# Squared-ReLU attention with a soft mixture of experts on one core: four relu buffers, the combine softmax in the logits' tile, and another order of loads and turns in the last chunks

## The chip, the cores and the metric

The kernel runs on one core of a Trainium2 chip. The time is device microseconds of one execution. Before the change the median of three runs is 1475.71 us (1475.2 to 1476.64). The profiled execution took 1476.88 us, and its span, from the first to the last instruction, is 1475.1 us: 1.8 us lie outside the span, and the profiled execution is 1.2 us above the median.

## The reference

```
scores = (z @ z.T) / S               # per batch: z is 2496 x 64, 8 batches
attn   = max(scores, 0) ** 2
x      = u * (attn @ v)              # 2496 x 256 per batch, 19968 tokens in all
logits = x @ phi                     # 19968 x 32, 8 experts with 4 slots each
d      = softmax of logits over the tokens     # one column per slot
slot_input = d.T @ x                 # 32 x 256
h      = max(slot_input[e] @ w1[e], 0)         # per expert, 256 -> 1024
slot_out[e] = h @ w2[e]                        # 1024 -> 256
c      = softmax of logits over the slots      # one row per token
out    = c @ slot_out                # 19968 x 256, float32
```

The softmax over the tokens is kept as a running maximum with rescaled sums, so that it can be added up while the tokens are still being made. The experts and the output need all tokens.

## The kernel before, in words

**Tiles.** Attention runs over 8 batches and, in each, over chunks of query tokens: five chunks of up to 512 tokens, and in the last batch chunks of 448, 512, 512, 512, 256 and 256. A chunk is named by its first token, so the last three are 18944 (512 tokens), 19456 and 19712 (256 tokens each). A chunk is five steps `p`, each over four blocks `kt` of 128 keys, and a step is two halves, which are called **slots** here: a chunk has ten slots. In each slot `between` runs first, then 24 matmuls `acc<-ph,v`, `acc<-pl,v` accumulate the chunk's output.

**What a slot carries.** `between` (L552) takes one task from the list `work`, then calls `pair`, which issues the scores of two key blocks for a slot three further on: six matmuls into two PSUM tiles `sc`, two relu on ACT into SBUF tiles `r` (L204), two squares in place, and on DVE per block a rounding copy `ph` and the rest `pl`. `run(middle)` (L207) puts pending ACT work between the relus and the squares, `run(behind)` (L216) puts pending DVE work behind the pair. Every engine executes in the order in which the program was written (`InOrder`), so this order is the schedule.

**The tasks.** 1024 finished tokens are a group `q` (0 to 19; group 18 is tokens 18432 to 19455, the last, 19, has 512). `groups(q)` (L303) returns its tasks: `blocks` turn the four quarters of `xg` into `y` (DVE `y<-xg`), `logits` runs matmuls `lg<-xg,phi_sb` and a DVE chain on `L`, with the exponentials `E` put in `middle`; `turn_e` turns `E` (DVE `y<-E`); four `shifts` are four DMAs each (`xt<-y`), issued by SP; `combine` and what follows make the softmax over the slots, the exponential again in `middle`; `slot_sums` multiplies the turned tokens, and `add_up` adds the product to `slot_acc` on DVE. In groups before 18 the sums ride with the next group's logits (`late`, `lg<-xt`). Group 18 is finished only when chunk 18944 is, so its tasks run one per slot through chunks 19456 and 19712. `between_last` (L518) turns part of the last tokens (`tr_last`) in the last two slots.

**Buffers and weights.** Keys and values of a batch take 15 of the 22 buffers of the pool `blk`. The expert weights are 32 tiles of 512 KB. Seven go to the buffers that are free in the last batch; eight follow in the last chunk, each into a block of keys or values that has been used up; ten go to a pool `wx` that takes over the space of the attention's working tiles, and seven more to `blk`. All DMAs are issued by SP, in program order, so a DMA that waits holds back all behind it.

**The end.** Behind the last chunk come the last group, layer 1 (`h<-w`), the turn of the hidden values (`hT`), layer 2 (`po<-w,hT`), and the output: 22 tiles `ot`, up to 1 MB each, made of `pf<-ch,soh` matmuls, copied by ACT and DVE and sent by SP (`outT<-ot`), 20.45 MB in all. The second half of layer 2 is spread among the first output tiles.

Of the kernel before, what the change touches and what calls it, by code (L numbers as in the profile page):

```python
# [8 lines left out]
F32 = mybir.dt.float32  # L9
# [7 lines left out]
P = 128  # L17
# [36 lines left out]
def attn_soft_moe_kernel(ctx, tc, uT, v, zz, phi, ww, outT):  # L54
# [125 lines left out]
    def scores(b, ch, p, w):  # L180


        j, o, n, t0 = ch
        k0 = 4 * p + 2 * w
        ps = [sc_ps.tile([P, QC], F32, tag="sc", name=f"sc_{t0}_{k0 + h}") for h in range(2)]
        if t0 == 0:
            for h, rows in enumerate(HALF):
                c = 2 * w + h
                pe.matmul(
                    ps[h], zraw[b, p][rows, c * P : (c + 1) * P], zraw[b, 0][rows],  # L190
                    start=True, stop=True,
                )
        else:
            zk, zq = zt[b, p], zt[b, j]
            for m, (kl, ql) in enumerate(((0, 0), (0, 1), (1, 0))):
                for h, rows in enumerate(HALF):
                    c = 2 * w + h
                    pe.matmul(
                        ps[h][:, :n], zk[rows, h ^ kl, c * P : (c + 1) * P],
                        zq[rows, h ^ ql, o : o + n], start=(m == 0), stop=(m == 2),  # L200
                    )
        rs = []
        for h in range(2):
            r = wa.tile([P, QC], F32, tag="r", name=f"r_{t0}_{k0 + h}", bufs=3)  # L204
# [61 lines left out]
    def finish_chunk(b, ch, acc):  # L266
        _, _, n, t0 = ch
        ut = ut_.pop(t0)
        s = 0
        while s < n:  # L270
            q, o = divmod(t0 + s, 1024)
            w = min(n - s, 1024 - o)
            if q not in xg_:
                xg_[q] = wk.tile([P, 2, 1024], F32, tag="xg", name=f"xg_{q}")
            for c in (slice(0, 1), slice(1, 2)) if t0 + n == N else (slice(0, 2),):
                dve.tensor_mul(xg_[q][:, c, o : o + w], acc[:, c, s : s + w], ut[:, c, s : s + w])
            if o + w == 1024:
                work.extend(groups(q))
            s += w

    late = []


    xt_last = [xt[:, t, 0:D] for t in range(4)]
# [18 lines left out]
    def groups(q):  # L303

        x = xg_.pop(q)
        L, E, lt = (
            wk.tile([P, 2 * P], F32, tag=t, name=f"{t}_{q}", bufs=1) for t in ("L", "E", "lt")
        )  # L310
        m = wk.tile([P, 5], F32, tag="m", name=f"m_{q}")
        rm = wk.tile([P, 2, 8], F32, tag="rm", name=f"rm_{q}")
        y = wk.tile([P, 4, NB], F32, tag="y", name=f"y_{q}", bufs=1)
        l8 = lt.rearrange("p (k s) -> p k s", s=NS)
        mnew, mold = runmax[q % 2], runmax[(q + 1) % 2]

        def logits():
# [10 lines left out]
                        )  # L328
            if late:
                late.pop()(ps)  # L330
            dve.tensor_copy(L, ps[:, 0, D : 2 * D])
            dve.tensor_add(L, L, ps[:, 1, D : 2 * D])
            if q == 0:
                dve.reduce_max(mnew, L, axis=AX.X)
            else:
                dve.reduce_max(m[:, 0:1], L, axis=AX.X)
                dve.tensor_max(mnew, m[:, 0:1], mold)
                dve.tensor_sub(m[:, 2:3], mold, mnew)
            dve.tensor_scalar_mul(m[:, 1:2], mnew, -1.0)
            middle.append(exps)  # L340

        def exps():
            act.activation(E, L, AF.Exp, bias=m[:, 1:2], accum_out=m[:, 4:5])
            if q:
                act.activation(m[:, 3:4], m[:, 2:3], AF.Exp)

# [1 line left out]

        def turn_block(j, c):
            dve.transpose(  # L350
                y[:, :, j * D : (j + 1) * D].rearrange("p b (t c f) -> p c t b f", t=4, c=2)[:, c],
                x[:, c, 512 * j : 512 * (j + 1)].rearrange("p (t b k) -> p t b k", t=4, b=4),
            )

        def turn_e():
            dve.transpose(
                y[:, :, 2 * D :].rearrange("p b (j s) -> p j b s", j=2),
                E.rearrange("p (j b k) -> p j b k", j=2, b=4),
            )


# [1 line left out]
            return rm[:, i].unsqueeze(2).to_broadcast([P, 8, NS])  # L363

        def combine():
            dve.transpose(lt, L)
            dve.tensor_reduce(rm[:, 0], l8, axis=AX.X, op=ALU.max)
            dve.tensor_sub(l8, l8, spread(0))

        def combine_exp():  # L370
            act.activation(lt, lt, AF.Exp)

        def combine_sum():
            dve.tensor_reduce(rm[:, 1], l8, axis=AX.X, op=ALU.add)
            dve.tensor_scalar_add(rm[:, 1], rm[:, 1], 1e-9)
            dve.reciprocal(rm[:, 1], rm[:, 1])
            dve.tensor_mul(l8, l8, spread(1))

        def combine_turn():
            dve.transpose(cw[:, 2 * q : 2 * q + 2].rearrange("p j n -> p (j n)"), lt)  # L380

        def slot_sums(ps):
            for j in range(2):
                for t in range(4):
                    o = 2 * D + j * NS
                    for h, rows in enumerate(HALF):
# [3 lines left out]
                            xt[rows, :, j * D + t * 64 : j * D + (t + 1) * 64],  # L390
                            start=(j == 0), stop=(j == 1),
                        )
            behind.append(lambda: add_up(ps))

        def add_up(ps):
            snew, sold = slot_acc[q % 2], slot_acc[(q + 1) % 2]
# [14 lines left out]
        shifts = [lambda a=a: shift(y, a) for a in range(4)]  # L411
        e, c0, c2, c3 = (lambda f=f: behind.append(f) for f in (turn_e, combine, combine_sum, combine_turn))
        c1 = lambda: middle.append(combine_exp)
        rest = lambda: None
        if q < NQG - 2:

            todo = [logits, *blocks, e, shifts[0], c0, shifts[1], c1, shifts[2], c2, shifts[3], c3]
            todo.append(lambda: late.append(slot_sums))
        else:


            todo = [*blocks[:2], logits, rest, *blocks[2:], e, *shifts, c0, c1, c2, c3, rest]
# [18 lines left out]
    def load_w(pool, tag):
        i = len(w_raw)
        if i < NW:
            t = pool.tile([P, 2, 512], F32, tag=tag, name=f"w_{i}")
            sp.dma_start(t, ww[i].rearrange("p (k n) -> p k n", k=2))
            w_raw.append(t)
# [35 lines left out]
    def loads(i, w):  # L482
# [6 lines left out]
        if b < B - 1:  # L489
            if j == NQ - 3 and w:  # L490
                landing.append(load_z(b + 1, p))
            m = -1
            if j == NQ - 2 and w:
                m = p - 1
            elif j == NQ - 1 and q in (1, 3, 5, 7, 8, 9):
                m = NQ - 1 + (1, 3, 5, 7, 8, 9).index(q)
            if m >= 0:
                landing.append(load_v(b + 1, m))
        elif t0 >= N - 512 - 256 and t0 < N - 256:
            if len(w_raw) < NBLK - 15:  # L500
                load_w(blk, "blk")
        elif t0 == N - 256 and q >= 2:
            load_w(blk, "blk")
        if i % (NQ * NP) == 0 and w == 0 and landing:
            behind.append(landing.pop(0))

# [6 lines left out]

        return opening_splits

    xps = []
# [31 lines left out]
    for i, (b, ch, p) in enumerate(steps):  # L548
# [315 lines left out]
```

## Time and profile before

| what | value |
|---|---|
| median of 3 runs | 1475.71 us |
| profiled execution | 1476.88 us |
| its span | 1475.1 us |
| PE busy | 1448.1 us, 98% |
| DVE busy | 1172.4 us, 79% |
| ACT busy | 980.7 us, 66% |
| weights `w<-in_w` | 32 DMAs of 512 KB |
| outputs `outT<-ot` | 22 DMAs of 512 KB to 1 MB |

The page's shares are means over stages that differ. Up to about 1354 us from the span's start the chunks have 512 queries; chunks 19456 and 19712 follow until 1397; layers 1 and 2 until about 1428; and the last 45 us are output. The change touches the stretch from about 1350 us on, so the views to read are those limited to a window there: the waits of each engine, the issues of SP, and the table of stretches with the share and the rate of the DMA engines. In a table of stretches the columns are the stretch and its length, busy time of each engine with the number of instructions, the granted TensorE clock, the share of time that the 16 DMA engines were busy, and GB/s. In a list of waits they are who waited for whom, the sum in us, how often, and the longest.

### The profile page before, as it was taken

The page shows a single profiled execution, that of the slowest core. Times are in us where ns is not written, and L with a number is a line of the kernel's source. Part 1 is how long each engine was busy: PE and PEld are TensorE (multiplying, and loading weights), DVE is VectorE, ACT ScalarE, POOL GpSimd, SP SyncE. Part 2 cuts the span into 40 slices and gives each one's busy share as a digit, 9 for nine tenths or more (in the row PEclk, how much of TensorE's full clock was granted, in tenths as well). Part 3 has the DMA queues.
Part 4 walks back from the last instruction along what each step waited for, and adds up shares of the span by engine and source line. Part 5 has one row for each costly group of instructions (what it writes and reads, how often), then busy time and mean ns, then how long its engine had stood idle before and what let it go on. Part 6 is the DMA issues. An engine that isn't in the chain of part 4 may idle for free.

```text
span 1475.1 us, 35858 instructions
## 1 busy us (share of the span) xinstructions
PE 1448.1 (98%) x13945; PEld 1206.1 (82%) x13945; DVE 1172.4 (79%) x2324; ACT 980.7 (66%) x1923; POOL 4.0 (0%) x22
## 2 busy tenths in 40 slices
PE   9999999999999999999999999999999999999985
PEld 6888989898987888789888888789888788878852
DVE  6878876888788887788778888798878888777754
ACT  7777766767667766677667676676767776655543
POOL 0000000000000000000000000000000000000000
PEclk9999999999999999999999999999999999999995
DMA  3013111132021302131112231121202130203599
GB/s 123 22 44 83 58 40 29 46 106 55 26 76 46 90 20 55 44 84 54 44 31 69 61 85 45 46 74 58 55 16 83 44 89 22 54 15 130 190 389 387
DMA packets 51243, 113.90 MB, mean 77 GB/s; under 512 B 8577, under 2 KB 11137, under 8 KB 49025
## 3 DMA queue, kind: packets, MB, share of 16 engines
q1 hardware_dynamic: 51072, 111.61, 24.2%
q8 instruction: 110, 1.80, 0.5%
q14 instruction: 61, 0.49, 0.1%
HBM read 68.71 MB, written 20.45 MB: 60 GB/s over the span
## 4 chain that ended last, share of the span: by engine, by line
PE 93%; DVE 3%; ACT 2%; DMA 1%; issue 1%; ACTq 0%; DVEq 0%; SPq 0%
PE acc L50 70%; PE sc L50 18%; PE lg L50 2%; PE pf L50 1%; ACT ot L50 1%; DMA w<-in_w 1%; DVE pl L50 1%; ACT r L50 1%; DVE ph L50 1%; PE h L50 0%; DMA outT<-ot 0%; DVE z L50 0%; DVE xg L50 0%; PE idle L50 0%; PE po L50 0%
## 5 line engine op out<-in xcount | busy, mean ns | idle before, releaser
L50 PE MATMUL acc<-ph,v 64*128 64x512 f32 (+2 forms) x6396 | 1023.7, 382 | 0.7 <-DVE v L50 0.6
L50 PEld LDWEIGHTS acc<-ph,v 64*128 64x128 f32 x6396 | 675.6, 184 | 102.9 <-issue 1.5
L50 ACT ACTIVATE r<-sc 128x512 f32<-128x512 f32 (+2 forms) x820 | 435.8, 574 | 435.0 <-PE sc L50 392.2
L50 PE MATMUL acc<-pl,v 64*128 64x512 f32 (+2 forms) x3198 | 696.2, 381 | 0.0
L50 DVE TENSOR_TENSOR pl<-r,ph 128x512 fp32r<-128x512 f32 (+5 forms) x820 | 546.3, 666 | 68.5 <-DVE ph L50 0.9
L50 DVE CAST ph<-r 128x512 fp32r<-128x512 f32 (+2 forms) x820 | 334.2, 408 | 158.8 <-ACT r L50 157.6
L50 ACT ACTIVATE r<-r 128x512 f32<-128x512 f32 (+2 forms) x820 | 454.4, 609 | 0.0
L50 PEld LDWEIGHTS acc<-pl,v 64*128 64x128 f32 x3198 | 374.2, 184 | 48.8
L50 PE MATMUL sc<-z,z 64*128 64x512 f32 (+2 forms) x1920 | 284.1, 382 | 1.2 <-ACT r L50 1.2
L50 PEld LDWEIGHTS sc<-z,z 64*128 64x128 f32 x1920 | 195.6, 185 | 41.6 <-issue 6.2
L50 PE MATMUL sc<-z 64*128 64x512 f32 (+2 forms) x480 | 70.3, 381 | 1.3 <-ACT r L50 1.3
L50 PEld LDWEIGHTS sc<-z 64*128 64x128 f32 x480 | 48.4, 185 | 10.2 <-ACT r L50 1.9
L50 DVE TENSOR_TENSOR v<-vr,v 128x512 fp32r<-128x512 f32 x80 | 53.5, 677 | 3.9 <-ACT v L50 3.7
L50 DVE STREAM_TRANSPOSE y<-xg 128x512 f32<-128x512 f32 x76 | 53.7, 706 | 0.6
L50 DVE TENSOR_TENSOR xg<-acc,ut 128x1024 f32<-128x1024 f32 (+7 forms) x57 | 48.8, 880 | 3.9 <-PE acc L50 3.9
L50 ACT CAST v<-vr 128x512 fp32r<-128x512 f32 x80 | 48.6, 617 | 2.1 <-DMA vr<-in_v 2.1
L50 DVE TENSOR_TENSOR z<-zr,z 64x512 fp32r<-64x512 f32 x70 | 48.0, 686 | 2.1
L50 ACT CAST z<-zr 64x512 fp32r<-64x512 f32 x70 | 43.4, 620 | 1.7
L50 DVE COPY ot<-pf 128x1024 f32<-128x1024 f32 (+2 forms) x22 | 24.3, 1104 | 23.0 <-PE pf L50 21.7
L50 ACT COPY ot<-pf 128x1024 f32<-128x1024 f32 (+2 forms) x22 | 20.1, 915 | 27.0 <-PE pf L50 25.5
L50 PE MATMUL pf<-ch,soh 32*128 32x512 f32 (+2 forms) x88 | 24.0, 596 | 10.4 <-ACT ot L50 10.3
L50 PEld LDWEIGHTS pf<-ch,soh 32*128 32x128 f32 x88 | 10.4, 252 | 22.0 <-ACT ot L50 20.2
(123 smaller groups left out, 376.8 us busy)
## 6 DMA issues: line engine op xcount, KB each, us to landing
xt<-y SPq DMA_DIRECT2D x304, 72.0 KB, 2.4
vr<-in_v SPq DMA_DIRECT2D x80, 256.0 KB, 3.4
w<-in_w SPq DMA_DIRECT2D x32, 512.0 KB, 8.5
outT<-ot SPq DMA_DIRECT2D x16, 1024.0 KB, 6.5
ut<-in_uT SPq DMA_DIRECT2D x31, 512.0 KB, 3.9
zr<-in_zz SPq DMA_DIRECT2D x35, 256.0 KB, 4.0
ut<-in_uT SPq DMA_DIRECT2D x8, 448.0 KB, 3.7
outT<-ot SPq DMA_DIRECT2D x4, 512.0 KB, 6.1
```

The source lines that it names most:

```text
L50: return lambda *a, **k: self.tc.keep_in_program_order(f(*a, **k))
```

## The change

Five edits. (1) The tiles `r` have four buffers where they had three. (2) The combine softmax works in `L` itself; the tile `lt` is gone, and `L`, `E`, `y` are allocated where they are first used. (3) Group 18 gets its tasks as soon as its first 512 tokens are finished, and the first two block turns go to the last two slots of chunk 18944; in turn the two last tasks of an earlier group are joined to one. Within chunk 19456 the order is now: pause, two block turns, pause, logits, pause, `turn_e`, shifts. (4) The sums of group 17 are added up behind the first shift, not behind the logits; those of group 18 are multiplied one slot sooner and added up a slot after that. (5) In the last chunk 13 blocks are taken for weights where it were 8, and they are loaded in the order of the table `w_order`, which is not the order of their numbers; the space `wx` then takes weights 20 to 29. The last tokens' first two turns go to PSUM tiles of the pool `sc`, where they went to the single tile of the pool `ms`.

```diff
-            r = wa.tile([P, QC], F32, tag="r", name=f"r_{t0}_{k0 + h}", bufs=3)
+            r = wa.tile([P, QC], F32, tag="r", name=f"r_{t0}_{k0 + h}", bufs=4)
...
             if o + w == 1024:
-                work.extend(groups(q))
+                work.extend(todo_.pop(q, None) or groups(q))
+            elif q == NQG - 2 and o + w == 512:
+
+                todo_[q] = groups(q)
+                work.extend([todo_[q].pop(0) for _ in range(2)])
             s += w
...
         def combine():
-            dve.transpose(lt, L)
-            dve.tensor_reduce(rm[:, 0], l8, axis=AX.X, op=ALU.max)
-            dve.tensor_sub(l8, l8, spread(0))
+            dve.transpose(L(), L())
+            dve.tensor_reduce(rm[:, 0], l8(), axis=AX.X, op=ALU.max)
+            dve.tensor_sub(l8(), l8(), spread(0))
...
-            behind.append(lambda: add_up(ps))
+            (behind if q < NQG - 3 else adding).append(lambda: add_up(ps))
...
-            todo = [logits, *blocks, e, shifts[0], c0, shifts[1], c1, shifts[2], c2, shifts[3], c3]
-            todo.append(lambda: late.append(slot_sums))
+            todo = [logits, *blocks, e, shifts[0], c0, shifts[1], c1, shifts[2], c2, shifts[3]]
+            todo.append(lambda: (c3(), late.append(slot_sums)))
         else:
-            todo = [*blocks[:2], logits, rest, *blocks[2:], e, *shifts, c0, c1, c2, c3, rest]
+            add = lambda: behind.append(adding.pop(0))
+            todo = [*blocks[:2], rest, *blocks[2:], rest, logits, rest, e, lambda: (shifts[0](), add()), *shifts[1:]]
+            todo += [c0, c1, c2, c3]
             todo.append(lambda: slot_sums(ms_ps.tile([P, 2, 512], F32, tag="ms", name=f"sl_{q}")))
+            todo.append(add)
...
+    NW0 = NBLK - 15
+    w_order = [(0,), (1,), (2,), (5, 6), (3,), (7, 8), (4,), (9, 10), (), (11, 12)]
...
-        elif t0 == N - 256 and q >= 2:
-            load_w(blk, "blk")
...
-        if k == 1:
-            xps.append(ms_ps.tile([P, 2, 512], F32, tag="ms", name="tr_last"))
         if k:
-            ps = xps[0][:, k - 1, 0:D]
+            ps = sc_ps.tile([P, QC], F32, tag="sc", name=f"tr_last_{k}")[:, 0:D]
...
             pair(i + 1, s)
+            if i >= len(steps) - NP:
+                if len(w_raw) == NW0:
+                    for _ in range(13):
+                        take_w(blk, "blk")
+                for k in w_order[2 * p + s]:
+                    load_w(NW0 + k)
...
-    for _ in range(NWX):
-        load_w(wx, "wx")
-    while len(w_raw) < NW:
-        load_w(blk, "blk")
+    for i in range(NW0 + 13, NW):
+        take_w(*((wx, "wx") if i < NW0 + 13 + NWX else (blk, "blk")))
+        load_w(i)
```

The queue of SP behind the last shift of group 18 and the last load of `ut`. In a row `w_7` is weight tile 7, and the brackets name the semaphores that the load waits for (`DMAHW` is a DMA eight issues earlier; `PE` the last matmul that read the block). Before:

```order
L50 DMA ut_19712_21109<-in_uT 128x2x256 [waits DMAHW0_49,DVE_49]
L50 DMA w_7_21111<-in_w 128x1024 [waits DMAHW1_49,PE_49]
L50 DMA w_8_21160<-in_w 128x1024 [waits DMAHW2_49,PE_49]
...
L50 DMA w_14_21483<-in_w 128x1024 [waits DMAHW0_49,PE_49]
L50 DMA w_15_21567<-in_w 128x1024 [waits DMAHW1_49,DVE_49,PE_49]
L50 DMA w_16_21569<-in_w 128x1024 [waits DMAHW2_49,DVE_49]
```

Now:

```order
L50 DMA ut_19712_21090<-in_uT 128x2x256 [waits DMAHW0_49,DVE_49]
...
L50 DMA w_9_21116<-in_w 128x1024 [waits DMAHW3_49,PE_49]
L50 DMA w_12_21119<-in_w 128x1024 [waits DMAHW4_49,PE_49]
L50 DMA w_13_21120<-in_w 128x1024 [waits DMAHW5_49,PE_49]
L50 DMA w_10_21117<-in_w 128x1024 [waits DMAHW6_49,PE_49]
...
L50 DMA w_15_21122<-in_w 128x1024 [waits DMAHW0_49,PE_49]
L50 DMA w_11_21118<-in_w 128x1024 [waits DMAHW1_49,PE_49]
L50 DMA w_16_21123<-in_w 128x1024 [waits DMAHW2_49,PE_49]
...
L50 DMA w_18_21125<-in_w 128x1024 [waits DMAHW4_49,PE_49,Activation_49]
L50 DMA w_19_21126<-in_w 128x1024 [waits DMAHW5_49,PE_49,Activation_49]
L50 DMA w_20_21559<-in_w 128x1024 [waits DMAHW6_49,DVE_49,PE_49]
```

The load that waits for the end of attention (on DVE and PE both) stood ninth behind `ut`; now it stands fourteenth, and the five that moved ahead of it wait for single blocks.

DVE around the finish of chunk 18944 (`xg_18<-acc_18944`) and up to the turn of the exponentials (`y_18<-E_18`), before; `y_18<-xg_18` is a block turn, `L_18<-lg_18` the copy of the logits, and the left-out rows are `ph` and `pl` of the blocks between, and short rows of the logits and the sum:

```order
L50 TENSOR_TENSOR xg_18_20066<-acc_18944_20068,ut_18944_20069 128x2x512
...
L50 STREAM_TRANSPOSE y_18_20563<-xg_18_20066 128x4x4x32
...
L50 STREAM_TRANSPOSE y_18_20563<-xg_18_20066 128x4x4x32
L50 COPY L_18_20558<-lg_18_20667 128x256
...
L50 SCALAR_TENSOR_TENSOR slot_acc1_84<-slot_acc0_83,m_17_19540,lg_18_20667 128x256
...
L50 STREAM_TRANSPOSE y_18_20563<-xg_18_20066 128x4x4x32
...
L50 STREAM_TRANSPOSE y_18_20563<-xg_18_20066 128x4x4x32
...
L50 STREAM_TRANSPOSE y_18_20563<-E_18_20559 128x2x4x32
```

Now:

```order
L50 STREAM_TRANSPOSE y_18_20473<-xg_18_20048 128x4x4x32
...
L50 STREAM_TRANSPOSE y_18_20473<-xg_18_20048 128x4x4x32
L50 TENSOR_TENSOR xg_18_20048<-acc_18944_20052,ut_18944_20053 128x2x512
...
L50 STREAM_TRANSPOSE y_18_20473<-xg_18_20048 128x4x4x32
...
L50 STREAM_TRANSPOSE y_18_20473<-xg_18_20048 128x4x4x32
...
L50 COPY L_18_20779<-lg_18_20746 128x256
...
L50 STREAM_TRANSPOSE y_18_20473<-E_18_20800 128x2x4x32
...
L50 SCALAR_TENSOR_TENSOR slot_acc1_84<-slot_acc0_83,m_17_19520,lg_18_20746 128x256
```

Two of the four block turns stand ahead of the finish of chunk 18944, all four ahead of the logits, and the rescaled sum of group 17 stands behind `y<-E`, where it stood ahead of it.

More of the change, by code (lines that the diff above doesn't have):

```diff
@@ L277, in finish_chunk @@
             if o + w == 1024:
-                work.extend(groups(q))
+                work.extend(todo_.pop(q, None) or groups(q))
+            elif q == NQG - 2 and o + w == 512:
+                todo_[q] = groups(q)
+                work.extend([todo_[q].pop(0) for _ in range(2)])
             s += w
-    late = []
+    late, adding, todo_ = [], [], {}
     xt_last = [xt[:, t, 0:D] for t in range(4)]
@@ L303, in groups, with own @@
     def groups(q):
[L307 to L310, printed above, removed]
+        x = xg_[q]
+        tiles = {}
+        def own(tag, *shape):
+            if tag not in tiles:
+                tiles[tag] = wk.tile([P, *shape], F32, tag=tag, name=f"{tag}_{q}", bufs=1)
+            return tiles[tag]
+        L, E, y = lambda: own("L", 2 * P), lambda: own("E", 2 * P), lambda: own("y", 4, NB)
         m = wk.tile([P, 5], F32, tag="m", name=f"m_{q}")
         rm = wk.tile([P, 2, 8], F32, tag="rm", name=f"rm_{q}")
-        y = wk.tile([P, 4, NB], F32, tag="y", name=f"y_{q}", bufs=1)
-        l8 = lt.rearrange("p (k s) -> p k s", s=NS)
+        l8 = lambda: L().rearrange("p (k s) -> p k s", s=NS)
         mnew, mold = runmax[q % 2], runmax[(q + 1) % 2]
@@ L330, in logits @@
                 late.pop()(ps)
-            dve.tensor_copy(L, ps[:, 0, D : 2 * D])
-            dve.tensor_add(L, L, ps[:, 1, D : 2 * D])
+            dve.tensor_copy(L(), ps[:, 0, D : 2 * D])
+            dve.tensor_add(L(), L(), ps[:, 1, D : 2 * D])
             if q == 0:
-                dve.reduce_max(mnew, L, axis=AX.X)
+                dve.reduce_max(mnew, L(), axis=AX.X)
             else:
-                dve.reduce_max(m[:, 0:1], L, axis=AX.X)
+                dve.reduce_max(m[:, 0:1], L(), axis=AX.X)
                 dve.tensor_max(mnew, m[:, 0:1], mold)
@@ L342, in exps @@
         def exps():
-            act.activation(E, L, AF.Exp, bias=m[:, 1:2], accum_out=m[:, 4:5])
+            act.activation(E(), L(), AF.Exp, bias=m[:, 1:2], accum_out=m[:, 4:5])
             if q:
@@ L350, in turn_block @@
             dve.transpose(
-                y[:, :, j * D : (j + 1) * D].rearrange("p b (t c f) -> p c t b f", t=4, c=2)[:, c],
+                y()[:, :, j * D : (j + 1) * D].rearrange("p b (t c f) -> p c t b f", t=4, c=2)[:, c],
                 x[:, c, 512 * j : 512 * (j + 1)].rearrange("p (t b k) -> p t b k", t=4, b=4),
@@ L356, in turn_e @@
             dve.transpose(
-                y[:, :, 2 * D :].rearrange("p b (j s) -> p j b s", j=2),
-                E.rearrange("p (j b k) -> p j b k", j=2, b=4),
+                y()[:, :, 2 * D :].rearrange("p b (j s) -> p j b s", j=2),
+                E().rearrange("p (j b k) -> p j b k", j=2, b=4),
             )
@@ L365, in combine @@
         def combine():
-            dve.transpose(lt, L)
-            dve.tensor_reduce(rm[:, 0], l8, axis=AX.X, op=ALU.max)
-            dve.tensor_sub(l8, l8, spread(0))
+            dve.transpose(L(), L())
+            dve.tensor_reduce(rm[:, 0], l8(), axis=AX.X, op=ALU.max)
+            dve.tensor_sub(l8(), l8(), spread(0))
         def combine_exp():
-            act.activation(lt, lt, AF.Exp)
+            act.activation(L(), L(), AF.Exp)
         def combine_sum():
-            dve.tensor_reduce(rm[:, 1], l8, axis=AX.X, op=ALU.add)
+            dve.tensor_reduce(rm[:, 1], l8(), axis=AX.X, op=ALU.add)
             dve.tensor_scalar_add(rm[:, 1], rm[:, 1], 1e-9)
             dve.reciprocal(rm[:, 1], rm[:, 1])
-            dve.tensor_mul(l8, l8, spread(1))
+            dve.tensor_mul(l8(), l8(), spread(1))
         def combine_turn():
-            dve.transpose(cw[:, 2 * q : 2 * q + 2].rearrange("p j n -> p (j n)"), lt)
+            dve.transpose(cw[:, 2 * q : 2 * q + 2].rearrange("p j n -> p (j n)"), L())
         def slot_sums(ps):
@@ L410, in groups @@
         blocks = [lambda j=j, c=c: behind.append(lambda: turn_block(j, c)) for j in range(2) for c in range(2)]
-        shifts = [lambda a=a: shift(y, a) for a in range(4)]
+        shifts = [lambda a=a: shift(y(), a) for a in range(4)]
         e, c0, c2, c3 = (lambda f=f: behind.append(f) for f in (turn_e, combine, combine_sum, combine_turn))
@@ L438, in split_lo, with take_w, load_w @@
         parts[k].append(lo)
[L441 to L446, printed above, removed]
+    def take_w(pool, tag):
+        w_raw.append(pool.tile([P, 2, 512], F32, tag=tag, name=f"w_{len(w_raw)}"))
+    def load_w(i):
+        sp.dma_start(w_raw[i], ww[i].rearrange("p (k n) -> p k n", k=2))
     w_raw = []
+    NW0 = NBLK - 15
+    w_order = [(0,), (1,), (2,), (5, 6), (3,), (7, 8), (4,), (9, 10), (), (11, 12)]
     def load_u(b, ch):
@@ L499, in loads @@
         elif t0 >= N - 512 - 256 and t0 < N - 256:
-            if len(w_raw) < NBLK - 15:
-                load_w(blk, "blk")
-        elif t0 == N - 256 and q >= 2:
-            load_w(blk, "blk")
+            if len(w_raw) < NW0:
+                take_w(blk, "blk")
+                load_w(len(w_raw) - 1)
         if i % (NQ * NP) == 0 and w == 0 and landing:
@@ L514, in loads @@
         return opening_splits
-    xps = []
     def between_last(k):
-        if k == 1:
-            xps.append(ms_ps.tile([P, 2, 512], F32, tag="ms", name="tr_last"))
         if k:
-            ps = xps[0][:, k - 1, 0:D]
+            ps = sc_ps.tile([P, QC], F32, tag="sc", name=f"tr_last_{k}")[:, 0:D]
             turn_x(ps, xg_[NQG - 1], k - 1)
@@ L556, in between @@
             pair(i + 1, s)
+            if i >= len(steps) - NP:
+                if len(w_raw) == NW0:
+                    for _ in range(13):
+                        take_w(blk, "blk")
+                for k in w_order[2 * p + s]:
+                    load_w(NW0 + k)
             if 2 * i + s + 3 >= 2 * len(steps):
@@ L572, in attn_soft_moe_kernel @@
     wx = exx.enter_context(tc.tile_pool(name="wx", bufs=NWX, side="right", reuse_waits="tile"))
-    for _ in range(NWX):
-        load_w(wx, "wx")
-    while len(w_raw) < NW:
-        load_w(blk, "blk")
+    for i in range(NW0 + 13, NW):
+        take_w(*((wx, "wx") if i < NW0 + 13 + NWX else (blk, "blk")))
+        load_w(i)
     q = NQG - 1
@@ L591, in attn_soft_moe_kernel @@
     E = wk.tile([P, 2 * P], F32, tag="E", name="E_last", bufs=1)[:, 0:P]
-    lt = wk.tile([P, 2 * P], F32, tag="lt", name="lt_last", bufs=1)[:, 0:P]
+    lt = wk.tile([P, 2 * P], F32, tag="L", name="lt_last", bufs=1)[:, 0:P]
     nc.gpsimd.memset(tiny[:, 0:512], 0.0)
@@ L602, in attn_soft_moe_kernel @@
     pm = sc_ps.tile([P, QC], F32, tag="sc", name="pm")
-    xq = ms_ps.tile([P, 2, 512], F32, tag="ms", name="tr_last_1")
+    xq = ms_ps.tile([P, 2, 512], F32, tag="ms", name="tr_last")
     ep_, tp = (acc_ps.tile([P, 2, QC], F32, tag="acc", name=n) for n in ("et_sums", "et_last"))
```

## The prediction

> **What bounds the kernel now.** The page first: PE is busy 98% of the span, so nearly all of it is matmuls at their own pace, and a gain is to be looked for only where that ends. The table of stretches (the columns are named in its head) shows where.
>
> ```profile
> core 0: us, PE busy (x) PEld busy (x) DVE busy (x) ACT busy (x) POOL busy (x), PEclk, DMA share, GB/s
> 1000.00:1300.00 300.00, 300.00 (x2915) 254.16 (x2913) 244.67 (x497) 201.75 (x402) 0.00 (x0) 1.00 0.18 51
> 1390.00:1395.00 5.00, 4.33 (x66) 3.79 (x64) 3.10 (x10) 1.66 (x5) 0.00 (x0) 1.00 1.02 396
> 1395.00:1400.00 5.00, 5.00 (x63) 3.82 (x59) 1.83 (x7) 1.21 (x5) 0.00 (x0) 1.00 0.77 277
> 1400.00:1405.00 5.00, 4.67 (x42) 2.29 (x44) 3.07 (x13) 2.82 (x7) 0.00 (x0) 1.00 0.92 325
> 1405.00:1410.00 5.00, 5.00 (x49) 1.31 (x41) 4.93 (x7) 3.85 (x6) 0.00 (x0) 1.00 1.03 417
> 1420.00:1425.00 5.00, 4.17 (x78) 2.50 (x74) 2.08 (x3) 1.66 (x3) 0.00 (x0) 1.00 0.86 345
> 1425.00:1430.00 5.00, 4.45 (x76) 2.64 (x71) 2.56 (x3) 2.72 (x3) 0.00 (x0) 1.00 0.91 375
> 1430.00:1435.00 5.00, 3.01 (x23) 1.62 (x24) 3.56 (x3) 2.62 (x4) 0.00 (x0) 0.76 1.01 418
> 1460.00:1465.00 5.00, 3.53 (x36) 1.97 (x28) 2.45 (x2) 2.09 (x3) 0.00 (x0) 0.50 1.00 415
> ```
>
> Up to 1300 us PE has no gap, and the edits that reach back there (the fourth buffer, the shared tile, the joined tasks) can win nothing in that part. From 1390 the DMA engines are full (share about 1, some 415 GB/s) but for two dips: at 277 and 325 GB/s they leave (138 + 90) / 415 x 5 = 2.7 us unused between 1395 and 1405, and at 345 and 375 another 1.3 us between 1420 and 1430. So the end is a DMA stage of weights and outputs, and two things set it: when SP can feed it, and when the first outputs are there. The issues of SP say why the first dip is there (start, length, what, how many):
>
> ```profile
> 1372.93 10.87 SPq L50 DMA_DIRECT2D xt<-y  x16
> ...
> 1383.90 0.53 SPq L50 DMA_DIRECT2D ut<-in_uT  x1
> 1384.53 4.63 SPq L50 DMA_DIRECT2D w<-in_w  x8
> ...
> 1397.37 7.03 SPq L50 DMA_DIRECT2D w<-in_w  x10
> ...
> 1424.93 0.33 SPq L50 DMA_DIRECT2D outT<-ot  x1
> ...
> SPq L50 <- DVE y L50: 13.3, 1, 13.3
> ```
>
> SP waits 13.3 us for `y`, then needs 10.87 us to issue 16 shifts, then sends eight weights by 1389.2 and nothing until 1397.37, the end of attention. Eight weights and `ut` are 4.5 MB, 11 us at 415 GB/s: they have run dry when the next ones come. Why `y` is late is in the groups and waits of DVE between 1354 and 1394, the two chunks of 256:
>
> ```profile
> L50 DVE TENSOR_TENSOR pl<-r,ph 128x256 fp32r<-128x256 f32 x33 | 14.0, 425 | 2.6
> L50 DVE CAST ph<-r 128x256 fp32r<-128x256 f32 x35 | 9.9, 283 | 2.7 <-ACT r L50 2.2
> L50 DVE STREAM_TRANSPOSE y<-xg 128x512 f32<-128x512 f32 x4 | 2.8, 705 | 0.0
> ...
> DVE ph L50 <- ACT r L50: 2.2, 4, 1.1
> ...
> ACT r L50 <- DVE pl L50: 3.4, 8, 0.8
> ACT lt L50 <- DVE lt L50: 1.5, 1, 1.5
> ...
> PE sc L50 <- ACT r L50: 1.4, 4, 0.5
> PE tr_last L50 <- DVE slot_acc L50: 0.6, 1, 0.6
> ...
> PE po L50 <- DMA w<-in_w: 1.7, 3, 0.8
> ```
>
> DVE waited only 2.2 us for relus and squares in these 40: it works back to back, and ACT (3.4 us in 8 waits) waits for it because a third relu tile is still being read. In this stretch DVE, not PE, sets the pace, and PE loses 1.4 us to relus and 0.6 to the sum of group 18.
>
> **The change part by part.** Sums are made against the profiled execution's own span, 1475.1 us; its time was 1476.88, and the median of the runs is 1475.71, so the change of the span is laid on the median.
>
> *Block turns and the late sum.* Before `y<-E` can run, DVE now has less ahead of it.
>
> ```profile
> 1353.07 0.30 DVE L50 CAST ph<-r 128x256 fp32r<-128x256 f32 x1 [1.46 <-ACT r L50]
> ...
> 1362.95 0.29 DVE L50 CAST ph<-r 128x256 fp32r<-128x256 f32 x1 [1.07 <-ACT r L50]
> ...
> 1364.29 0.47 DVE L50 SCALAR_TENSOR_TENSOR slot_acc<-slot_acc,m,lg 128x256 f32<-128x256 f32 x1
> ...
> 1364.81 0.42 DVE L50 TENSOR_TENSOR slot_acc<-slot_acc,lg 128x256 f32<-128x256 f32 x1
> 1365.14 0.29 DVE L50 CAST ph<-r 128x256 fp32r<-128x256 f32 x1
> ...
> 1372.43 0.45 DVE L50 STREAM_TRANSPOSE y<-E 128x256 f32<-128x256 f32 x1
> ```
>
> The first turn falls into the 1.46 us that DVE idles before 1353.07; of the second the cover is gone, since it stands in the back-to-back stretch, ahead of `xg`. That takes 0.70 us off the stretch. The sum of group 17 (1364.29 to 1365.14: 0.85 us with its small third part) moves behind `y<-E`. Together `y` is ready 1.55 us sooner. The shifts keep their 10.87 us, so `ut` and the first weight follow 1.55 us sooner. What is late next: the sum, one chunk on, has nobody waiting for it until group 18's. The logits come two slots later with the same chain and the same 1.07 us of DVE idle behind the exponentials: no gain, no loss, as `y<-E` stands two slots behind them still.
>
> *Four relu tiles.* The trace has no run with four. The bounds are 0 (DVE, with the same work, takes the time back) and the whole 1.4 us that PE waited for relus. I take 0.95: the waits behind the two exponentials remain in part, because ACT's 1.5 us for the combine (`lt`, now `L`) is a chain of dependent steps and not a lack of tiles.
>
> *The last tokens' turn* in the `sc` tiles no longer waits for `slot_acc`: 0.55 us (the row gives 0.6). So attention ends 0.70 + 0.95 + 0.55 = 2.2 us sooner, 0.55 at the least, 3.0 at the most (0.70 + 1.4 + 0.55, and a third of a us of short DVE waits).
>
> *Slot sums a slot sooner.* PE runs them in order, and they need the last shift. It is issued at 1383.1 (the end of the 16, less a sixteenth of 10.87) and lands 2.4 us later by the row `xt<-y` of the page's issues; 1.55 us sooner that is 1383.95, and the slot starts at 1386.34 less 0.70 and 0.95, 1384.7. It lies free by 0.7 us; without the earlier `y` PE would wait 0.8.
>
> ```profile
> xt<-y SPq DMA_DIRECT2D x304, 72.0 KB, 2.4
> ...
> 1386.34 0.62 PE L50 MATMUL sc<-z,z 64*128 64x256 f32 x6
> ```
>
> *Weights.* Thirteen instead of eight between the shifts and the end of attention, in the order in which blocks come free: the loads behind them no longer find a dry queue, and the 2.7 us dip is filled. A load whose block is late holds back the others, but with seven free at once (9 us of transfers) it has time. The weights are all there 1.55 + 2.7 = 4.25 us sooner. Sharing `L` and joining two tasks cost no instruction: nothing, below the matmuls.
>
> *From the end of attention to the outputs* the instructions are the same. Layer 2 waited three times, 1.7 us, for weights (row above); weights that come 4.25 us sooner for work that is 2.2 us sooner are there. So the third output, from which on the rate stays at 415 GB/s, is issued 2.2 + 1.7 = 3.9 us sooner than 1424.93. From there the stage is as long as it was: the second dip, before that output, stays. The chain of transfers (4.25) allows it, the chain of computation (3.9) decides: **1475.7 - 3.9 = 1471.8 us**.
>
> **The rivals.** *DVE keeps the pace.* If the fourth relu tile gives nothing and the block turn only moves the wait, attention ends 0.55 us sooner and the third output 2.25: 1473.5. For it: DVE's sum of work falls by only 0.70 us. Against it: waits of ACT on `pl` are eight, and spread. *The weights cover more.* If all of PE's waits go and attention ends 3.0 us sooner, the output is 4.7 sooner and the transfers' 4.25 decide, less a part of the second dip, which weights then fill: some 4.9, 1470.8, and at best with all of that dip 1470.2. *The shifts are not sooner* (PE or ACT is behind `y<-E`, not DVE): the queue starts as before, the slot sums wait 0.8 us, attention ends 1.4 us sooner, and the transfers gain 2.7 only: 1473.0.
>
> *Slower: the clock falls before the outputs begin.* The granted clock is 1.00 to 1430, 0.76 in the stretch from 1430 and 0.50 behind it, with PE busy 3.01 of 5 us where it falls. PE now gets less to wait for before the outputs, but comes to the sparse stage sooner. These rows lie between attention and the outputs:
>
> ```profile
> 1402.29 1.92 PE h L50 x16
> ...
> 1404.78 5.33 PE h L50 x48
> ...
> 1410.00 1.97 PE L50 MATMUL hT<-ident,hidden 128*128 128x128 f32 x16
> ...
> 1411.89 3.70 PE L50 MATMUL po<-w,hT 128*32 128x128 f32 x128
> ```
>
> At half the clock they would take up to 12.9 us more, 1471.8 + 12.9 = 1484.7; it decides from 3.9 us of them on, when the gain is eaten. Against it: the clock stayed at 1.00 through all of this stage. The Trainium skill, "TensorE: Matmul & The Clock Gate", Part 1, has the clock halve after one window of about 3.4 us in which PE idles and come back after one busy window. By that rule this rival needs such an idle window, and the rows show PE busy over half of every stretch, so it would not happen; but by these same rows the fall at 1430 to 1435 came with PE busy 3.01 of 5, so the trace does not bear the rule out as a full account.
>
> **How the numbers follow.** Forecast 0.55; weights cover more 0.16; DVE keeps the pace 0.12; shifts not sooner 0.10; slower, the clock or another loss of the same size, 0.07. A change under 0.2%, 2.95 us, can't be told from none here, which puts the line at 1472.8. Faster: the forecast, with a part of its spread beyond the line counted off, and the stronger case, 0.69; same: the two weak cases and that part, 0.24; slower 0.07. The range for 8 in 10 goes from 1469.4 (the strong case and 0.8 us for the spread of runs) to 1474.3 (both weak cases and 0.8).
>
> **What would show it.** Right: `y<-E` about 1.5 us before 1372.43 and the shifts with it; 13 weights between `ut` and the end of attention and no stretch of 5 us under 380 GB/s from 1387 to 1415; attention's last matmul about 2 us before 1397.3; no wait of `po` for `w`; fewer waits of ACT on `pl`; the third output near 1421. Wrong: `sl` waiting for `xt`; a new wait of SP for a block ahead of weights that are free; weights done well before the first output, with the DMA engines idle for longer than the second dip; a clock below 1.00 before 1420.

## The result, and the profile after

The changed kernel takes 1467.02 us (median of six runs, 1466.37 to 1467.45) where the kernel before took 1475.9 us beside it: a ratio of 0.9938, with a 95% interval of 0.9925 to 0.9951. That is 8.9 us, where 3.9 were forecast, and 1467.02 lies below the low end of the range. The profiled execution took 1466.37 us with a span of 1464.3. The spans differ by 10.8 us, 1.9 more than the medians, mostly since the profiled execution before lies 1.0 us above its median and the one after 0.65 below. One run of an experiment below, 1769.27 us at a granted clock of 0.747 where all other runs have 0.985 to 0.987, is left out of its ratio (the median there is 1472.48 with it and 1472.44 without).

The largest part of the 8.9 us was won before the place at which the prediction began to look. The timeline of PE shows the first scores of chunk 19456, with which the chunks of 256 queries begin; first the kernel before (start, length, what, how many), then the changed one:

```profile
1354.25 0.52 PE L50 MATMUL sc<-z,z 64*128 64x256 f32 x6
```

```profile
1348.13 0.52 PE L50 MATMUL sc<-z,z 64*128 64x256 f32 x6
```

These six matmuls come 6.12 us sooner. In the chunks of 512 little has changed: the number of relu tiles, the place of the combine softmax, and two tasks that are joined. The waits of ScalarE from 0 to 1300 us say what went away (engine, tile and whom it waited for: us in all, times, longest). Before:

```profile
ACT r L50 <- PE sc L50: 366.0, 311, 3.7
ACT r L50 <- DVE pl L50: 30.9, 48, 2.0
ACT r L50 <- PE acc L50: 3.0, 3, 1.6
```

After:

```profile
ACT r L50 <- PE sc L50: 401.0, 324, 3.5
```

With three tiles a relu had to wait 48 times, 30.9 us together, until VectorE had read the tile of three relus ago (`pl<-r,ph` is its last reader). With four there is no such wait. Most of them cost PE little or nothing, since scores are issued three slots ahead; some reach PE. One place shows how. The timeline before, from 290 to 299 us, of ScalarE, VectorE and PE (in square brackets the idle time before, and what ended it):

```profile
293.53 0.60 ACT L50 ACTIVATE r<-sc 128x512 f32<-128x512 f32 x1 [0.39 <-PE sc L50]
296.11 0.60 ACT L50 ACTIVATE r<-sc 128x512 f32<-128x512 f32 x1 [1.97 <-DVE pl L50]
```

```profile
292.44 0.44 DVE L50 STREAM_TRANSPOSE lt<-L 128x256 f32<-128x256 f32 x1
292.91 0.42 DVE L50 TENSOR_REDUCE rm<-lt 128x8 f32<-128x256 f32 x1
293.37 0.42 DVE L50 TENSOR_TENSOR lt<-lt,rm 128x256 f32<-128x256 f32 x1
293.71 1.22 DVE L50 TENSOR_TENSOR xg<-acc,ut 128x1024 f32<-128x1024 f32 x1
294.85 0.42 DVE L50 CAST ph<-r 128x512 fp32r<-128x512 f32 x1
295.30 0.69 DVE L50 TENSOR_TENSOR pl<-r,ph 128x512 fp32r<-128x512 f32 x1
```

```profile
292.64 0.96 PE L50 MATMUL sc<-z,z 64*128 64x512 f32 x6
...
296.14 0.39 PE L50 MATMUL sc<-z,z 64*128 64x512 f32 x1
296.76 0.96 PE L50 MATMUL sc<-z,z 64*128 64x512 f32 x5 [0.23 <-ACT r L50]
297.34 0.84 PE L50 MATMUL acc<-ph,v 64*128 64x512 f32 x4
```

At the end of a chunk VectorE has 2.4 us of other work in one piece (three steps of a combine softmax and `xg`, 292.44 to 294.9). It reads the old relu tile only from 294.85 to 295.99; the second relu of the pair, which could have followed the first at about 294.1, begins at 296.11; and the next scores, which need its PSUM tile, stop after one matmul. From the start of these six to the `acc` behind them are 1.20 us. The same place after the change:

```profile
292.71 0.63 PE L50 MATMUL acc<-ph,v 64*128 64x512 f32 x4
293.18 0.39 PE L50 MATMUL acc<-pl,v 64*128 64x512 f32 x2
293.41 0.86 PE L50 MATMUL sc<-z,z 64*128 64x512 f32 x6
294.11 0.63 PE L50 MATMUL acc<-ph,v 64*128 64x512 f32 x4
```

```profile
290.81 1.09 ACT L50 ACTIVATE r<-sc 128x512 f32<-128x512 f32 x2 [1.36 <-PE sc L50]
294.30 1.08 ACT L50 ACTIVATE r<-sc 128x512 f32<-128x512 f32 x2 [1.37 <-PE sc L50]
```

There it is 0.70 us, and both relus of a pair follow each other. The scores of this slot were 2.73 us sooner than before (293.41 for 296.14), the matmuls behind them are 3.23 sooner (294.11 for 297.34): one stall of 0.5 us. Of it the timeline counted 0.23 as a wait, and for all of 0 to 1300 us the waits of PE before give no more than this:

```profile
PE sc L50 <- ACT r L50: 1.0, 4, 0.3
```

What PE lost stands in another row, the waits of its weight loads (PEld) for the same relus, from 0 to 1300 us. Before, and after:

```profile
PEld sc L50 <- ACT r L50: 5.7, 13, 0.8
```

```profile
PEld sc L50 <- ACT r L50: 0.5, 2, 0.3
```

Three of the 13 and both of the two lie in the first 10 us. The other ten, 4.7 us in all, are at ten places between 55 and 1055 us, and with four tiles none of them is left. A single wait is not the exact loss: at 296.76 us the weight load waited 0.66 us where PE lost 0.5.

The lead of matching scores grows in such steps and some smaller ones: 2.2 us by 62 us of the kernel before, 2.7 by 262, 3.9 by 400, 5.0 by 745, 5.5 by 991, 6.1 by 1090. The first part of it is not won by the tiles. Some 0.8 us are there before a third relu has been issued; the second row of matmuls on `idle`, before and after, shows it:

```profile
5.84 1.03 PE L50 MATMUL idle<-cw 64*128 64x512 bf16 x8
```

```profile
5.05 1.03 PE L50 MATMUL idle<-cw 64*128 64x512 bf16 x8
```

In the eight experiments below this row begins anywhere from 4.86 to 5.86 us, the earliest with three tiles and one of the two latest with four, so it does not go with the number of tiles. From this row to the first scores of chunk 19456 it is 1348.3 to 1348.5 us in the four profiled executions with three tiles in the chunks of 512 (the kernel before among them), and 1343.0 to 1343.1 in the six with four or five. So the traces give the fourth tile 5.3 of the 6.12 us.

The rows by stretch, after (PE, PEld, DVE, ACT, POOL busy, then the granted clock, the DMA share, GB/s):

```profile
1000.00:1300.00 300.00, 300.00 (x2918) 248.63 (x2916) 244.87 (x495) 200.91 (x402) 0.00 (x0) 1.00 0.18 50
1385.00:1390.00 5.00, 5.00 (x74) 4.09 (x72) 1.72 (x6) 0.74 (x2) 0.00 (x0) 1.00 1.04 420
1390.00:1395.00 5.00, 4.56 (x49) 2.61 (x45) 2.96 (x14) 2.05 (x8) 0.00 (x0) 1.00 1.01 403
1410.00:1415.00 5.00, 4.82 (x100) 2.88 (x96) 2.37 (x4) 2.17 (x4) 0.00 (x0) 1.00 0.82 324
1415.00:1420.00 5.00, 4.07 (x74) 2.63 (x68) 3.62 (x3) 2.77 (x3) 0.00 (x0) 1.00 1.02 420
1420.00:1425.00 5.00, 2.85 (x34) 1.74 (x28) 2.65 (x3) 2.56 (x4) 0.00 (x0) 0.92 1.01 416
```

The first row is busy for 300.00 of 300 us, as it was before, though 0.6 us were won in that stretch. The first dip of the transfers is gone (every stretch between 1385 and 1410 has 403 GB/s or more); of the second (415 - 324) / 415 x 5 = 1.1 us are left.

The issues of SP from 1365 us on, in two windows, and the waits of PE from 1340 to 1465:

```profile
1365.25 10.64 SPq L50 DMA_DIRECT2D xt<-y  x16
1375.98 0.53 SPq L50 DMA_DIRECT2D ut<-in_uT  x1
1376.61 26.70 SPq L50 DMA_DIRECT2D w<-in_w  x25
1410.47 1.69 SPq L50 DMA_DIRECT2D outT<-ot  x2
...
1414.16 4.32 SPq L50 DMA_DIRECT2D outT<-ot  x3
```

```profile
PE pf L50 <- ACT ot L50: 11.1, 16, 0.9
PE po L50 <- ACT so L50: 1.2, 1, 1.2
PE sc L50 <- ACT r L50: 0.7, 1, 0.7
PE h L50 <- ACT tiny L50: 0.3, 1, 0.3
```

The shifts begin 7.68 us sooner (1365.25 for 1372.93), 1.56 more than the scores of chunk 19456. The third output, 1414.16, is 10.77 us sooner: 6.12 up to the first scores of chunk 19456, the 0.8 of the opening among them, and 4.65 from there on, where the forecast had 3.9. PE waits neither for weights in `po` nor for the sum of group 18 in `tr_last`.

### The profile page after: what moved, and what is told of

It is laid out like the page before. It is cut to its first block, busy times and chain, and to the rows that moved or that the text cites. A ratio compares the mean times of both kernels' runs of the same rounds, so it can differ in the third digit from the quotient of the medians.

```text
span 1464.3 us, 35841 instructions
## 1 busy us (share of the span) xinstructions
PE 1440.0 (98%) x13945; PEld 1169.9 (80%) x13945; DVE 1169.8 (80%) x2324; ACT 975.0 (67%) x1923; POOL 3.8 (0%) x22
## 4 chain that ended last, share of the span: by engine, by line
PE 96%; DMA 1%; DVE 1%; ACT 1%; issue 0%; ACTq 0%; DVEq 0%; SPq 0%; POOLq 0%
PE acc L50 72%; PE sc L50 19%; PE lg L50 2%; PE pf L50 1%; DMA outT<-ot 1%; ACT ot L50 1%; PE po L50 1%; PE h L50 0%; DVE pl L50 0%; PE idle L50 0%; DVE ot L50 0%; DVE ph L50 0%; ACT r L50 0%; PE hT L50 0%; PE et_sums L50 0%
## 5 line engine op out<-in xcount | busy, mean ns | idle before, releaser
L50 PE MATMUL acc<-ph,v 64*128 64x512 f32 (+2 forms) x6396 | 988.5, 382 | 0.7 <-DVE v L50 0.6
L50 ACT ACTIVATE r<-sc 128x512 f32<-128x512 f32 (+2 forms) x820 | 428.1, 574 | 432.4 <-PE sc L50 430.8
L50 PEld LDWEIGHTS acc<-ph,v 64*128 64x128 f32 x6396 | 605.2, 184 | 122.1 <-POOLq L253 1.4
L50 PE MATMUL acc<-pl,v 64*128 64x512 f32 (+2 forms) x3198 | 626.1, 381 | 0.0
L50 PEld LDWEIGHTS acc<-pl,v 64*128 64x128 f32 x3198 | 310.2, 184 | 57.9
L50 PE MATMUL sc<-z,z 64*128 64x512 f32 (+2 forms) x1920 | 265.2, 380 | 0.0
L50 PEld LDWEIGHTS sc<-z,z 64*128 64x128 f32 x1920 | 178.7, 184 | 41.1 <-issue 6.2
L50 PE MATMUL sc<-z 64*128 64x512 f32 (+2 forms) x480 | 66.6, 381 | 0.7 <-ACT r L50 0.7
L50 PEld LDWEIGHTS sc<-z 64*128 64x128 f32 x480 | 44.5, 184 | 10.8 <-issue 2.1
```

The source lines that it names most:

```text
L50: return lambda *a, **k: self.tc.keep_in_program_order(f(*a, **k))
```

## The experiments

Two theories stood before the first four. **A**: the fourth relu tile wins most of the time, in the chunks of 512 queries. **B**, the prediction's account: nothing is won there, and the gain is that of the last chunks. All times are medians, all ratios are to the kernel before on the same chip. An interval reaches 0.0008 to 0.0014 to either side, 1.2 to 2 us, so a difference of less than about 2 us between two changed kernels lies within the intervals and is told with the trace beside it.

| kernel | time, us | ratio, 95% interval |
|---|---|---|
| the change | 1467.02 | 0.9938, 0.9925 to 0.9951 |
| change, three relu tiles | 1473.61 | 0.9983, 0.9975 to 0.9992 |
| before, softmax in `L` | 1476.16 | 0.9999, 0.9990 to 1.0008 |
| before, softmax in `L`, four relu tiles | 1468.83 | 0.9953, 0.9939 to 0.9966 |
| change, eight weights as before | 1468.63 | 0.9949, 0.9936 to 0.9961 |
| change, fourth tile in the last chunks only | 1472.48 | 0.9973, 0.9964 to 0.9982 |
| change, old order of tasks | 1467.76 | 0.9945, 0.9933 to 0.9958 |
| change, last tokens' turns as before | 1467.11 | 0.9942, 0.9929 to 0.9956 |
| change, five relu tiles, nine `pl` | 1466.95 | 0.9940, 0.9927 to 0.9952 |

**Three relu tiles in the changed kernel**, all else as changed.

```diff
-            r = wa.tile([P, QC], F32, tag="r", name=f"r_{t0}_{k0 + h}", bufs=4)
+            r = wa.tile([P, QC], F32, tag="r", name=f"r_{t0}_{k0 + h}", bufs=3)
```

> The changed kernel with three relu tiles again, all else kept. Theory A: the fourth tile takes away ACT's waits for DVE in the chunks of 512 too (in the trace before, 31.2 us in 50 waits of ACT on pl up to 1340 us; in the trace after, none), and that is where 6.1 us of the gain lie, with some 1 us more in the chunks of 256. So 1467.0 + 7 = 1474 us, and the first scores of chunk 19456 come at about 1354 us from the span's start, not at 1348. Theory B, the prediction's own: the fourth tile is worth 0.95 us and the 6.1 us come from something else of the change, the shared tile or the joined tasks: 1468 us.

1473.61 us: one number takes back 6.6 of the 8.9 us, as A has it. The wait of ScalarE from 0 to 1300 us is back word for word:

```profile
ACT r L50 <- DVE pl L50: 30.9, 48, 2.0
```

and the scores of chunk 19456 begin at 1354.32, where they began before the change.

**The shared tile alone**: the kernel before, with the combine softmax in `L`.

```diff
-        L, E, lt = (
-            wk.tile([P, 2 * P], F32, tag=t, name=f"{t}_{q}", bufs=1) for t in ("L", "E", "lt")
-        )
+        L, E = (wk.tile([P, 2 * P], F32, tag=t, name=f"{t}_{q}", bufs=1) for t in ("L", "E"))
+        lt = L
...
-    lt = wk.tile([P, 2 * P], F32, tag="lt", name="lt_last", bufs=1)[:, 0:P]
+    lt = wk.tile([P, 2 * P], F32, tag="L", name="lt_last", bufs=1)[:, 0:P]
```

> The kernel before with the combine softmax in the logits' tile alone; three relu tiles. Theory A: the same instructions on the same engines, no time: 1475.9 us, within 1 us. Theory B: if the shared tile carries the 6.1 us (fewer tiles, other waits), 1469.8 us.

1476.16 us, a ratio of 0.9999: no time. The tile's 1 KB per partition is what it gives: the pool of the attention's tiles takes 52 KB per partition with four relu tiles (8 for `r`, 20 each for `ph` and `pl`, 4 for `ut`), and 51.09 KB are left for it before, 52.09 with the tile shared. So this edit wins nothing and the largest gain needs its room.

**Four relu tiles alone**: the kernel of the last experiment, with `bufs=4` in the line of the first.

> The kernel before with the shared tile and four relu tiles; tasks, sums, weights as before. Theory A: 6.1 us in the chunks of 512 and about 1 us in those of 256: 1468.9 us, that is more than three quarters of the whole gain from one number. Theory B: 1475.

1468.83 us. Of the whole change this number alone gives 7.1 us, 0.5 more than it takes back when it is undone, which is within the intervals. All other edits together add 1.8 us to it. PE still waits 0.8 us for weights in `po` there.

**Eight weights as before**: the changed kernel, with the loads of the last chunk in the old number and order (the inverse of the diff's edits at `load_w` and `w_order`).

> The changed kernel with the weights as before: eight blocks in the last chunk in the order of their numbers, then ten tiles at the end of attention, then seven blocks. Theory A: the transfers' dip of 2.7 us comes back, layer 2 waits for weights again, and the outputs start 1.7 to 2.5 us later: 1469 us. Theory C: the computation decides and hides it: 1467.

1468.63 us, 1.6 more than the change. By stretch:

```profile
1385.00:1390.00 5.00, 5.00 (x70) 4.09 (x70) 1.73 (x6) 0.74 (x2) 0.00 (x0) 1.00 0.93 375
1390.00:1395.00 5.00, 4.57 (x49) 2.78 (x45) 2.94 (x15) 2.05 (x8) 0.00 (x0) 1.00 0.84 256
```

```profile
PE po L50 <- DMA w<-in_w: 1.1, 2, 0.6
```

The first dip is back ((415 - 375 + 415 - 256) / 415 x 5 = 2.4 us), and so are two waits for weights. Both are what the prediction said of the weights. The 1.6 us are within the intervals, but no run of either kernel falls among those of the other (1466.37 to 1467.45 and 1468.21 to 1469.09).

**The fourth tile in the last two chunks only.** Now the place of the gain was to be shown by a time and not by a trace alone. In the chunks of 512 three tiles go round; in those of 256 every fourth relu has a tile of its own.

```diff
-            r = wa.tile([P, QC], F32, tag="r", name=f"r_{t0}_{k0 + h}", bufs=4)
+            if t0 >= N - QC and (k0 + h) % 4 == 3:
+                r = wa.tile([P, QC // 2], F32, tag="rx", name=f"r_{t0}_{k0 + h}", bufs=1)
+            else:
+                r = wa.tile([P, QC], F32, tag="r", name=f"r_{t0}_{k0 + h}", bufs=3)
```

> The changed kernel, with three relu tiles in the chunks of 512 columns and a fourth only in the last two chunks of 256. Theory A (most of the fourth tile's gain is made in the chunks of 512, where the relu waits for a tile that VectorE still reads): the time goes back by what three tiles everywhere cost (1473.6 against 1467.0, 6.6 us) less the part in the chunks of 256 (with four tiles alone the scores lie 6.0 us sooner at 1090 us and the end of attention 7.3 sooner, so 1.3): 1467.0 + 6.6 - 1.3 = 1472.3. In the trace 40 or so waits of ScalarE on pl before 1300 us, and the first scores of chunk 19456 within 0.3 us of 1354.25. Theory B (the prediction: nothing is to be had up to 1300 us, the fourth tile counts in the chunks of 256): within 0.5 us of 1467.0.

1472.48 us, where A expected 1472.3 and B 1467.0. So the fourth tile is worth 1472.48 - 1467.02 = 5.5 us in the chunks of 512, and 1473.61 - 1472.48 = 1.1 us in those of 256. ScalarE's waits from 0 to 1300 us and PE's first scores of chunk 19456:

```profile
ACT r L50 <- DVE pl L50: 31.0, 48, 2.0
```

```profile
1354.29 0.52 PE L50 MATMUL sc<-z,z 64*128 64x256 f32 x6
```

**The old order of tasks** in the changed kernel: block turns, logits and the sums of groups 17 and 18 where they were.

```diff
-            elif q == NQG - 2 and o + w == 512:
-
-                todo_[q] = groups(q)
-                work.extend([todo_[q].pop(0) for _ in range(2)])
...
-            (behind if q < NQG - 3 else adding).append(lambda: add_up(ps))
+            behind.append(lambda: add_up(ps))
...
-            todo = [*blocks[:2], rest, *blocks[2:], rest, logits, rest, e, lambda: (shifts[0](), add()), *shifts[1:]]
-            todo += [c0, c1, c2, c3]
+            todo = [*blocks[:2], logits, rest, *blocks[2:], e, *shifts, c0, c1, c2, c3, rest]
```

> The changed kernel with the order of tasks of before in the last chunks: turns of blocks, logits and the sums of groups 17 and 18 where they were; four relu tiles, the shared tile, the weights' order, the slot sums a slot sooner and the last turns are kept. Prediction's step: y<-E and the shifts 1.55 us later, PE waits 0.8 us for the last shift before the slot sums, attention ends 0.7 to 1.5 us later: 1467.0 + 1.1 = 1468.1. Rival (the end is set by the transfers, and with thirteen weights sent before the end of attention the queue has 1.5 us to spare): 1467.0 to 1467.3, though the trace shows the shifts later.

1467.76 us, 0.7 more than the change; neither account hit it. The edit also puts the multiplication of group 18's sums back by a slot (`sl<-xt` starts at 1381.6 us, where it started at 1378.8), which the expectation meant to keep; so the 0.8 us that PE was to wait for the last shift could not show, and there is no such wait. The profiled execution's first scores of chunk 19456 come at 1348.98 for 1348.13, 0.85 us later, 0.80 of it from the opening (5.86 for 5.05), before any edited task; what is beyond that comes from the tasks. SP and PE:

```profile
1367.42 11.08 SPq L50 DMA_DIRECT2D xt<-y  x16
```

```profile
PE po L50 <- DMA w<-in_w: 0.7, 1, 0.7
```

The shifts begin 1367.42 - 1365.25 - 0.85 = 1.3 us later than in the change, near the 1.55 of the prediction. But attention ends only 0.15 us later (1390.08 against 1389.08, less 0.85). The loss is in `po`, which waits 0.7 us for a weight again. So, in this trace, the earlier tasks pay through the weights that follow the shifts, and not through the end of attention. At 0.7 us against intervals of 2 us this reading rests on one trace.

**The last tokens' first two turns** back in the tile that waits for the sum of group 18.

```diff
+    xps = []
...
-            ps = sc_ps.tile([P, QC], F32, tag="sc", name=f"tr_last_{k}")[:, 0:D]
+            if k == 1:
+                xps.append(ms_ps.tile([P, 2, 512], F32, tag="ms", name="tr_first"))
+            ps = xps[0][:, k - 1, 0:D]
```

> The changed kernel with the first two turns of the last tokens back in the tile that waits for the sum of group 18. Prediction's step: PE waits 0.55 us for slot_acc again, attention's end and the first output are 0.55 us later: 1467.6. Rival (this wait is cover for another, or the transfers decide): 1467.0, with the wait in the trace and the third output within 0.2 us of 1414.16.

```profile
PE tr_first L50 <- DVE slot_acc L50: 0.5, 1, 0.5
```

The wait is back, and in the trace attention's end (1389.76 for 1389.08), the first output (1411.12 for 1410.47) and the third (1414.89 for 1414.16) are 0.65 to 0.73 us later, as the prediction has it. The median, 1467.11, is 0.1 us above that of the change. Whether this edit is worth 0.1 or 0.6 us these runs can't tell.

**Five relu tiles**, with nine `pl` instead of ten to make room.

```diff
-            r = wa.tile([P, QC], F32, tag="r", name=f"r_{t0}_{k0 + h}", bufs=4)
+            r = wa.tile([P, QC], F32, tag="r", name=f"r_{t0}_{k0 + h}", bufs=5)
...
-            lo = wa.tile([P, QC], F32R, tag="pl", name=f"pl_{t0}_{kt}", bufs=10)
+            lo = wa.tile([P, QC], F32R, tag="pl", name=f"pl_{t0}_{kt}", bufs=9)
```

> The changed kernel with five relu tiles and, for room, nine tiles pl instead of ten. Theory A (the cost is ScalarE's wait for a tile that VectorE still reads, and no such wait is left with four): no gain, within 0.4 us of 1467.0, unless the missing tile pl costs, which would show as a wait of VectorE on PE. Rival (four tiles only shortened what five would end, or the gain comes from another thing than this wait): 1464 to 1466.

1466.95 us: no gain, none lost. The waits of ScalarE from 0 to 1300 us are those of the change:

```profile
ACT r L50 <- PE sc L50: 401.5, 324, 3.5
```

VectorE waits a little more for PE at the nine `pl` (1.8 us up to 1340 us, where it was 1.0), but the scores of chunk 19456 come no later, counted from the second `idle` row. The cost was the wait for the third tile's reader; with four tiles it has ended. No version tried beats the change by more than these runs can tell.

## Why the prediction was wrong

The sum of the single measurements (the first two share one measured difference of 6.6) is 5.5 (fourth tile, chunks of 512) + 1.1 (fourth tile, chunks of 256) + 1.6 (weights) + 0.7 (tasks) + 0.1 (last turns) + 0 (shared tile) = 9.0 us, against 8.9 for the whole. The prediction's sum had 0 + 0.95 + 1.7 + 0.70 + 0.55 + 0 = 3.9.

- **The step that failed** is the second sentence of the reading of the first table: "Up to 1300 us PE has no gap, and the edits that reach back there (the fourth buffer, the shared tile, the joined tasks) can win nothing in that part." It was drawn from one row, PE busy 300.00 of 300.00 us. The fourth tile won 5.5 us there by the times, 5.3 by the traces. A busy PE in that row is no PE at its pace: the stretch from 290 to 302 us, before and then after, shows it 11.77 of 12 us busy with 102 matmuls and 12.00 with 106. PE lost 0.5 us there, and the row shows 0.23.

```profile
290.00:302.00 12.00, 11.77 (x102) 10.56 (x100) 10.97 (x21) 8.44 (x17) 0.00 (x0) 1.00 0.43 121
```

```profile
290.00:302.00 12.00, 12.00 (x106) 9.66 (x104) 11.32 (x22) 8.64 (x17) 0.00 (x0) 1.00 0.54 154
```

  The view that shows the loss was read, but only in a window: the prediction quotes ScalarE's waits on `pl` between 1354 and 1394 us (3.4 us, 8 times) and never asked for the same row from 0 to 1300 (30.9 us, 48 times), nor for the waits of the weight loads on relus (5.7 us, 13 times).

  That the rows of PE mislead here has a rule: the Trainium skill, "Perfetto Trace Analysis", section "Identifying the Most-Contended Engine", calls the matmuls' busy share a bad measure of how near a kernel is to its limit, and names two others instead: the share of the peak arithmetic rate that is reached, and the busy share of the weight loads. Its first half agrees with these rows. Of the two, the busy share of the weight loads would not have helped: the next column has the loads of the kernel before, which stalls, busy 10.56 us (100 of them) and those of the change 9.66 (104).

- **Four relu tiles, 0.95 us** was counted for the last chunks alone, and there it was right: 1.1. So were its mechanism and what was to remain (PE's 0.7 us behind an exponential).
- **Block turns and the late sum**: `y<-E` was to be ready 1.55 us sooner. Beside the 6.12 us it is 1372.43 - 1364.74 - 6.12 = 1.57. The sum of group 17 runs behind it, as forecast:

```profile
1364.74 0.45 DVE L50 STREAM_TRANSPOSE y<-E 128x256 f32<-128x256 f32 x1
...
1366.54 0.47 DVE L50 SCALAR_TENSOR_TENSOR slot_acc<-slot_acc,m,lg 128x256 f32<-128x256 f32 x1
```

  The 0.70 us that this was to give the end of attention has the right size by the times (0.7) only by luck: it came another way, through the weights. What the slot sums a slot sooner are worth was not tried by itself.
- **Attention ends 2.2 us sooner**: 8.26 measured (1389.08 for 1397.34), less 6.12 is 2.1. That the sum is this near is luck in part: from the first scores of chunk 19456 to the end of attention, the single edits undone cost 1.2 us (tile), 0.6 (last turns) and 0.15 (tasks), where 0.95, 0.55 and 0.70 were counted.
- **Weights**: the first dip is filled, the three waits of `po` are gone, and undone they cost 1.6 us for the 1.7 forecast. The second dip stays at 1.1 us for the 1.3 named.
- **The third output** was to be 3.9 us sooner. Beside the 6.12 it is 4.65, so that `po` and the first outputs gave 2.5 us where 1.7 were counted. By the medians, less 5.5, the last chunks gave 3.4 us. The 3.9 lies between the two.
- **The rivals.** That DVE keeps the pace fell, as ScalarE's waits on `pl` are gone. That weights cover more fell, since the second dip stays. The shifts are sooner. The clock is 1.00 up to 1420 us and 0.92 in the stretch behind it, after the first outputs: the slower case did not come. No rival had the fourth tile winning outside the last chunks, so the range had no room for it.

So 48 waits of ScalarE, 31 us in all, cost PE 5.5 us by the times and 5.3 by the traces, the opening taken off. Ten places show in the waits of its weight loads. What stays open is which waits make the smaller steps of the lead: only one place has been followed from engine to engine.

## What to carry to other kernels

A row that shows PE busy all the time does not show that it loses nothing: here matmul lengths, whose ends are modelled, covered more than half of a stall of 0.5 us. To see what a buffer more can win, read the waits of the engine that fills the buffer, over the whole span and not only where the change seems to act, and then the waits of PE's weight loads on that engine: their 5.2 us less were near what was won. Before a lead is read off two traces, take off what their openings differ by. An edit that saves no instruction can be worth what its bytes make room for.

## What the runs showed of the hardware

The busy time of PE's weight loads rises where PE stalls: 106 ns for one in the stretch from 290 to 302 us before (10.56 us, 100 loads), 93 ns after (9.66, 104). And ScalarE, which is busy only two thirds of the span, delayed PE through one tile of 256 KB: with three of them 1473.61 us, with four 1467.02, with five 1466.95.
